# A Trainium2 kernel of attention and two mixtures of experts: routing pieces in another order, and the last slot's logits worked out from SBUF

## The chip, the cores and the metric

The kernel runs on one core of one Trainium2 chip. The metric is device time in microseconds (us). Three runs of the kernel before gave 686.45, 686.72 and 690.42 us, median 686.72. Engines: PE multiplies matrices (its weight loads, PEld, overlap), ACT, DVE and POOL do elementwise work, SP starts loads and stores. Each engine runs its instructions strictly in the order in which they are written.

## The reference

Linear attention with 128 random features, then two routed layers with one expert per token:

```
h = x @ omega.T - sum(x*x)/2          # for q and k, scaled
phi = exp(h - max(h)) / sqrt(128)
out = phi_q @ (phi_k.T @ v) / (phi_q @ sum(phi_k) + 1e-6)
# out as x [2304, 512]; then twice:
logits = x @ w_gate (+ modality_bias[modality_id] in the second)
e = argmax(logits);  gate = softmax(logits)[e]
x = gate * (relu(x @ w1[e]) @ w2[e])  # w1 [512, 1024], w2 [1024, 512], 8 experts
```

## The kernel before

Each float32 operand of a matmul is split into a hi part (a cast, on ACT, sometimes POOL) and a lo part (a subtraction, on DVE, sometimes POOL: `fp32_parts`, L40 and L41), and a product is three matmuls: hi x hi, hi x lo, lo x hi.

**Attention** runs over eight groups (a pair of batches and a pair of heads) in numbered steps. `split(gi, which, c)` (L244) makes the parts of chunk c of q or k of group gi; for group 0 the hi part is on ACT, and the lo part on DVE if the chunk is listed in FIRST, else on POOL; all later groups are on POOL. `at(step, ...)` puts a piece into a step. `st_proj` (L274) projects on PE (L283 to L285), DVE takes maxima (L287), ACT exponentials (L292: `ek` for k, `eq` for q). The pieces of MoE 1's routing run in steps of the last groups; the last batch pair's first piece is `r1_a(1)` (choice of the expert, one-hot `oh`, count `S`), after which the pools of attention are closed and those of the MoEs opened.

**Each MoE** (`moe(m)`, m = 0 and 1) sorts its tokens by expert into slots of 128 tokens: 19 slots are used in MoE 1 (18 plus the last, in `rest`), 20 in MoE 2. For a slot s of the loop PE does `layer1(s)` (24 matmuls, L819 to L821), `tx(s+1)` (transposes of the next slot's tokens into `px`, L802, whose parts are `xh`, `xl`), `layer2(s-1)` (24 matmuls, L852 to L854, with an optional piece `mid` before one of its eight steps) and `th(s)` (eight transposes of relu's result `hr` into `ht`, L835, whose parts are `hh`, `hl`). `renew` splits the next expert's weights (`w1h`, `w1l`, `w2h`, `w2l`) where a flag says that the expert changes, and loads further ones into `raw`. `gather` (L745) fetches a slot's tokens by the index `idx` on POOL's queue; a slot's result is stored by SP (MoE 1) or scattered by POOL (MoE 2).

**Routing of MoE 2** is worked out during MoE 1: `logits_v` (five experts, DVE, from PSUM, L877), `logits_g` and `logits_s` (three experts, products on POOL, L885, sums on ACT, L891); for batches of slots `r2_a` (choice), `r2_b` (ranking matmuls `pm` by `rank_mm`, L696), `r2_c` and so on. A list `todo` with `put` and `work` spreads these over the slots. `early_table` (L561) makes a short table of the first slots' tokens from `er` (the result of `early_rhs`, L529), from which the first tokens of MoE 2 are gathered. The whole table comes in pieces: `final_1` (ranks), `final_2` and `final_4` (operands `R` on DVE), `final_3` (first part of the table: indices; "payload") and `final_5` (the rest: gates and output rows).

At the end of MoE 1 a branch on `go` runs `rest`: layer 1 of MoE 2's slot 0, the last layer 2 of MoE 1 and then the logits of that slot. The next work of PE, `layer1(1, 1)`, reads parts that either side of the branch has written, so it waits until ACT and DVE have come to the end of the branch.

## Time and profile before

| what | value |
|---|---|
| median of three runs | 686.72 us |
| the profiled execution: its own time, its span | 683.77 us, 682.1 us |
| mean granted TensorE clock | 0.979 |
| PE busy | 644.0 us, 94% |
| DVE, ACT, POOL busy | 381.3, 316.0, 236.3 us |
| mean rate of the DMA engines | 107 GB/s |

In the rows further down a timeline row is: start, length, engine, line, operation, result <- operands, shape, count, and in brackets the idle time of the engine just before it with what ended it ("issue" is a wait for nothing that the profile shows, "DVEq L785" DVE's own branch). [...]

### The profile page before, as it was taken

To read this page: it belongs to the slowest core of one execution; us is meant where nothing else is said; L and a number is where in the kernel's file an instruction comes from. 1 tells how busy PE (TensorE), PEld (TensorE's weight loads), DVE (VectorE), ACT (ScalarE), POOL (GpSimd) and SP (SyncE) were. 2 spreads that over 40 slices of the span, in tenths; PEclk is the share of its full clock that TensorE was granted. 3 is DMA by queue.
4 is the path that set the end of the run, shared out by engine and by line. 5 is a ranking of instruction groups with operands and counts; after the bars stand their busy time and mean duration, and the time that the engine had idled before them with its cause. 6 is when DMAs were issued, how large, how long until landed. Compare 5 with 4: busy or idle time off the path is not lost. (4 is left out here: it accounts for less than half of the span.)

```text
span 682.1 us, 12235 instructions
## 1 busy us (share of the span) xinstructions
PE 644.0 (94%) x3764; PEld 554.9 (81%) x3764; DVE 381.3 (56%) x966; ACT 316.0 (46%) x742; POOL 236.3 (35%) x284
## 2 busy tenths in 40 slices
PE   7999999998999999999999677999999999999994
PEld 6999999886877888888888565787888888888883
DVE  3666689968587844575777468275211441564110
ACT  5666766663135734435654147212122542574231
POOL 5967665570253443523424224002121121211101
PEclk9999999998999999999999789899999999999998
DMA  6385446254165421011100801005411441550000
GB/s 201 111 268 174 140 129 217 71 181 160 39 229 193 160 85 47 32 48 47 45 27 32 297 28 36 5 32 206 152 39 42 155 157 38 170 168 19 33 17 28
DMA packets 38769, 72.64 MB, mean 107 GB/s; under 512 B 4478, under 2 KB 19966, under 8 KB 38528
## 3 DMA queue, kind: packets, MB, share of 16 engines
q1 hardware_dynamic: 33856, 57.23, 24.6%
q0 software_dynamic: 4720, 14.16, 6.3%
q8 instruction: 35, 0.57, 0.4%
q14 instruction: 78, 0.64, 0.3%
q10 hardware_dynamic: 80, 0.03, 0.0%
HBM read 55.95 MB, written 16.78 MB: 107 GB/s over the span
## 5 line engine op out<-in xcount | busy, mean ns | idle before, releaser
L819 PE MATMUL ph<-w1h,xh 128*128 128x512 f32 x312 | 127.3, 408 | 5.7 <-ACT prod L891 5.7
L852 PE MATMUL py<-w2h,hh 128*128 128x512 f32 x312 | 127.4, 408 | 0.7 <-issue 0.7
L820 PE MATMUL ph<-w1h,xl 128*128 128x512 f32 x312 | 123.6, 396 | 1.4 <-DVE xl L41 0.7
L854 PE MATMUL py<-w2l,hh 128*128 128x512 f32 x312 | 124.1, 398 | 0.0
L821 PE MATMUL ph<-w1l,xh 128*128 128x512 f32 x312 | 123.9, 397 | 0.0
L853 PE MATMUL py<-w2h,hl 128*128 128x512 f32 x312 | 123.0, 394 | 0.0
L41 DVE TENSOR_TENSOR hl<-ht,hh 128x512 fp32r<-128x512 f32 x78 | 50.3, 685 | 119.2 <-ACT hh L40 117.1
L885 POOL TENSOR_TENSOR prod<-y,wg2b 128x512 f32<-128x512 f32 x54 | 68.9, 1301 | 127.7 <-ACT prod L891 127.7
L826 ACT ACTIVATE hr<-ph 128x512 f32<-128x512 f32 x78 | 42.3, 594 | 128.2 <-PE ph L821 120.1
L860 ACT ACTIVATE y<-py,gate 128x512 f32<-128x512 f32 x36 | 24.7, 687 | 134.7 <-PE py L854 134.7
L865 POOL DMA_INDIRECT out<-y,oid x18 | 19.2, 1065 | 182.8 <-ACT y L860 178.7
L41 DVE TENSOR_TENSOR xl<-px,xh 128x512 fp32r<-128x512 f32 x40 | 27.6, 691 | 95.4 <-ACTq L785 59.5
L819 PEld LDWEIGHTS ph<-w1h,xh 128*128 128x128 f32 x312 | 59.9, 192 | 17.2 <-ACT prod L891 5.9
L877 DVE CUSTOM_DVE_ANT_0 junk<-py,wg2b,gate 128x512 f32<-128x512 f32 x95 | 71.2, 749 | 2.9 <-DVEq L785 0.2
L820 PEld LDWEIGHTS ph<-w1h,xl 128*128 128x128 f32 x312 | 60.0, 192 | 13.6 <-DVE xl L41 1.1
L821 PEld LDWEIGHTS ph<-w1l,xh 128*128 128x128 f32 x312 | 59.7, 191 | 13.3
L854 PEld LDWEIGHTS py<-w2l,hh 128*128 128x128 f32 x312 | 59.4, 190 | 13.3
L853 PEld LDWEIGHTS py<-w2h,hl 128*128 128x128 f32 x312 | 59.8, 192 | 11.9
L852 PEld LDWEIGHTS py<-w2h,hh 128*128 128x128 f32 x312 | 59.7, 191 | 11.8 <-issue 0.8
L292 ACT ACTIVATE eq<-p,mxq 128x128 f32<-128x128 f32 x144 | 41.4, 373 | 41.0 <-DVE mxq L287 41.0
L40 ACT CAST hh<-ht 128x512 fp32r<-128x512 f32 x78 | 41.8, 590 | 4.5 <-issue 4.3
L292 ACT ACTIVATE ek<-p,mxk 128x128 f32<-128x128 f32 x144 | 42.1, 392 | 3.1 <-DVE mxk L287 3.1
(227 smaller groups left out, 1127.3 us busy)
## 6 DMA issues: line engine op xcount, KB each, us to landing
raw<-w SPq DMA_DIRECT2D x56, 512.0 KB, 5.4
rawk<-kT SPq DMA_DIRECT2D x24, 192.0 KB, 3.7
rawv<-v SPq DMA_DIRECT2D x8, 576.0 KB, 5.3
rawq<-qT SPq DMA_DIRECT2D x24, 192.0 KB, 5.3
xall<-xg SPq DMA_DIRECT2D x8, 576.0 KB, 3.3
y<-y SPq DMA_DIRECT2D x18, 256.0 KB, 2.0
wg2b<-wg SPq DMA_DIRECT2D x1, 2048.0 KB, 7.0
y<-xb SPq DMA_DIRECT2D x7, 256.0 KB, 3.5
```

The lines of the kernel that those rows point to most:

```text
L40: engine_hi(hi, x)
L41: engine_lo.tensor_tensor(out=lo, in0=x, in1=hi.bitcast(F32), op=ALU.subtract)
L292: nc.scalar.activation(e[:, u], p[:, u // 2, (u % 2) * 128:(u % 2) * 128 + 128], AF.Exp, bias=mx[:, u:u + 1], scale=1.0)
L819: nc.tensor.matmul(ph[:, n], h[:, k], self.w1h[k][:, c], start=(k == 0), stop=False)
L820: nc.tensor.matmul(ph[:, n], l[:, k], self.w1h[k][:, c], start=False, stop=False)
L821: nc.tensor.matmul(ph[:, n], h[:, k], self.w1l[k][:, c], start=False, stop=(k == 3))
L826: nc.scalar.activation(r[:, n * 512:n * 512 + 512], ph[:, n], AF.Relu)
L852: nc.tensor.matmul(py, h[:, k], wh, start=(k == 0), stop=False)
L853: nc.tensor.matmul(py, l[:, k], wh, start=False, stop=False)
L854: nc.tensor.matmul(py, h[:, k], wl, start=False, stop=(k == 7))
L877: nc.vector.tensor_tensor_reduce(out=self.junk, in0=py, in1=self.wg2b[:, e], op0=ALU.mult, op1=ALU.add, scale=self.gate[0][:, s:s + 1], sc ...
L885: nc.gpsimd.tensor_tensor(out=self.prod[e - NEV], in0=y, in1=self.wg2b[:, e], op=ALU.mult)
```

## The change

At the start of attention the third split of group 0's k is written one step later, and the first split of group 1's k goes from POOL, at step 2, to ACT and DVE at step 4. The pools of attention are closed after the first part of `r1_a(1)` (it is a generator, cut by a `yield`), and the rest of it is written behind. In MoE 1 two of the four splits of w2 are written behind `th(0)`; flags and the logits of slot 0 change places, `final_2` goes to slot 1, `final_5` into the middle of a layer 2. `early_rhs` and `early_table` go some slots later, the `big` flag is loaded for fewer engines (for PE one slot later, with `go`), and `split_first` stands behind `tx(19)`. The logits of the last slot leave the branch: the new `logits_last` works out all eight on DVE from `ylast` in SBUF, behind MoE 2's `th(0)`, into `lastl`, and `r2_a(2)` adds them to the row that a one-hot `llo` picks. In MoE 2, `r2_a`, `final_1`, `final_2`, `final_3` with the gathers, and the flags each stand about one slot sooner, and `tx(4)` is at its usual place again.

The diff, cut to its core:

```diff
-        FIRST = [("k", 0), ("k", 2), ("q", 1)]
+        FIRST = [(0, "k", 0), (0, "k", 2), (0, "q", 1), (1, "k", 0)]
...
-            if gi == 0:
-
-                fp32_parts(nc, nc.scalar.copy, nc.vector if (which, c) in FIRST else nc.gpsimd, h, l, t)
+            if gi == 0 or (gi, which, c) == (1, "k", 0):
+
+                fp32_parts(nc, nc.scalar.copy, nc.vector if (gi, which, c) in FIRST else nc.gpsimd, h, l, t)
             else:
                 fp32_parts(nc, pool_copy, nc.gpsimd, h, l, t)
             parts[gi, which, c] = h, l
...
-        for c in range(3):
+        for c in range(2):
             split(0, "k", c)
...
         fill_v(0)
+        at(0, split, 0, "k", 2)
         for c in range(3):
             at(c + 1, split, 0, "q", c)
...
-                        at(s + d, split, g + 1, which, c)
+                        at(4 if (g, which, c) == (0, "k", 0) else s + d, split, g + 1, which, c)
...
+    def logits_last(self):
+
+        with self.tc.If(self.nsv > NS0):
+            for e in range(NE):
+                self.nc.vector.tensor_tensor_reduce(
+                    out=self.junk, in0=self.ylast, in1=self.wg2b[:, e], op0=ALU.mult, op1=ALU.add,
+                    scale=1.0, scalar=0.0, accum_out=self.lastl[:, e:e + 1])
+
+        if b == 2:
+
+            nl = NSLOT - NS0
+            nn = sm.tile([128, 1], F32, tag="lln", name="lln", bufs=1)
+            lo = sm.tile([128, nl], F32, tag="llo", name="llo", bufs=1)
+            lt = sm.tile([128, nl, NE], F32, tag="llt", name="llt", bufs=1)
+            nc.vector.tensor_reduce(out=nn, in_=self.kept["nb_0"], axis=AX.X, op=ALU.add)
+            nc.vector.tensor_scalar(out=lo, in0=self.i25[:, NS0:], scalar1=nn[:, 0:1], scalar2=-1.0,
+                                    op0=ALU.subtract, op1=ALU.is_equal)
+            nc.vector.tensor_tensor(
+                out=lt, in0=self.lastl.rearrange("p (o e) -> p o e", o=1).to_broadcast([128, nl, NE]),
+                in1=lo.rearrange("p (t o) -> p t o", o=1).to_broadcast([128, nl, NE]), op=ALU.mult)
+            nc.vector.tensor_tensor(out=self.lg2[:, NS0:], in0=self.lg2[:, NS0:], in1=lt, op=ALU.add)
...
-        self.all(self.r1_a(1, lgp))
+        r1 = self.r1_a(1, lgp)
+        next(r1)
         actx.close()
...
+        self.all(r1)
 
         self.moe(0)
         self.moe(1)
...
     def early_gathers(self, m):
-        self.big[m], self.bigv[m] = (self.nc.values_load(
-            self.bigi[m], engines=e, min_val=0, max_val=1, skip_runtime_bounds_check_because="a flag")
-            for e in (ALL, VEC))
+        def load(engines):
+            return self.nc.values_load(self.bigi[m], engines=engines, min_val=0, max_val=1,
+                                       skip_runtime_bounds_check_because="a flag")
+
         if m == 0:
+            self.big[m] = load(ALL)
             self.gather(m, 0, early=True)
-        else:
-            self.go = self.nc.values_load(self.goi, engines=ALL, min_val=0, max_val=1,
-                                          skip_runtime_bounds_check_because="a flag")
-        with self.tc.If(self.big[m] > 0):
+        self.bigv[m] = load(VEC)
+        with self.tc.If(self.bigv[m] > 0):
             for s in range(1 - m, NEARLY[m]):
                 self.gather(m, s, early=True)
...
             with late.Else():
-                self.layer1(m, 0, after=[lambda: split2(0, 1), lambda: self.r1_b(1), self.r1_d,
-                                         lambda: split2(2, 3)])
+                self.layer1(m, 0, after=[lambda: split2(0, 1), lambda: self.r1_b(1), self.r1_d])
                 self.tx(m, 1)
         self.th()
         if m == 0:
+            split2(2, 3)
             if_big(self.final_1, m)
+        else:
+            if_big(self.logits_last, vec=True)
         self.reload(m, 0, 1, 3)
...
-            with when(s) as there:
-                first = []
-                if (m, s) != (1, 3):
-                    first.append(lambda: self.renew(m, s + 1, 0))
-                if m == 0 and s == NS0:
-                    first.append(lambda: self.split_first(s))
-                self.layer1(m, s, after=first)
-            if m == 0 and s == NS0:
-                with there.Else():
-                    self.split_first(s)
-            if s == 4 + m:
+            with when(s):
+                self.layer1(m, s, after=[lambda: self.renew(m, s + 1, 0)])
+            if s == 5 and m == 1:
                 if_big(self.final_5, m)
-            if (m, s) == (1, 2):
-                if_big(self.final_1, m)
-            if (m, s) == (1, 3):
-                rows()
             if s > 2 * m + 1:
                 with when(s + 3):
                     self.gather(m, s + 3)
-            if (m, s) != (1, 3):
-                self.tx(m, s + 1)
-            if (m, s) == (0, 1):
+            self.tx(m, s + 1)
+            if m == 0 and s == NS0:
+                self.split_first(s)
+            if s == 1 + m:
                 if_big(self.final_2, m, vec=True)
-            if (m, s) == (1, 3):
-                flags()
-                self.renew(m, s + 1, 0)
+            if (m, s) == (1, 1):
+                if_big(self.r2_a, 2, vec=True)
+            if (m, s) == (0, 2):
+                self.logits_v(0)
             if m == 0:
                 work(s, 4.6 if 2 < s < NS0 else 0)
+                if s == NS0:
+
+                    self.big[1], self.go = (self.nc.values_load(
+                        x, engines=ALL, min_val=0, max_val=1, skip_runtime_bounds_check_because="a flag")
+                        for x in (self.bigi[1], self.goi))
 
             def renew2():
                 with when(s):
                     self.renew(m, s, 1)
 
-            self.layer2(m, s - 1, mid={(0, NS0): (4, self.tx, 1, 0), (1, 3): (6, self.tx, 1, 4)}.get((m, s)),
+            self.layer2(m, s - 1, mid={(0, NS0): (4, self.tx, 1, 0), (0, 4): (4, if_big, self.final_5, 0)}.get((m, s)),
                         after=[renew2] if s > 1 else [])
             if (m, s) == (0, 1):
                 rows()
-            if (m, s) == (1, 3):
-                self.gather(m, 6)
             with when(s):
                 self.th()
             if s == 1:
                 self.renew(m, s, 1)
             if (m, s) == (1, 1):
-                if_big(self.r2_a, 2, vec=True)
+                if_big(self.final_1, m)
             if (m, s) == (1, 2):
-                if_big(self.final_2, m, vec=True)
-            if m == 0:
+                rows()
+                self.gather(m, 6)
+            if s == 1 + m:
+                flags()
+            if m == 0 and s > 1:
                 self.logits_v(s - 1)
-            if (m, s) == (0, 1):
-                flags()
             if s in (2 + m, 3 + m):
...
                 if s == EARLY + 1:
                     put(s + 1, 2, lambda: self.all(self.first_expert(1, self.live["tot2"])))
-                    put(s + 1, 1.8, e_rhs)
-                    put(s + 1, 2.1, lambda: self.all(rhs[0]))
-                    put(s + 2, None, e_table)
+                    put(s + 3, 1.8, e_rhs)
+                    put(s + 3, 2.1, lambda: self.all(rhs[0]))
                 work(s, 0)
                 if s == NS0 - 2:
 
-                    while "er" not in self.live:
+                    while todo and todo[0][0] <= s:
                         work(s, 1e3)
                     with tc.If(self.flag(0, 5, s, [ET.SP]) < 1):
                         self.first_weights(1)
+                if s == NS0 - 1:
+                    while "er" not in self.live:
+                        work(s, 1e3)
+                    self.early_table(1, self.A2, self.live["er"], EARLY)
+                    self.early_gathers(1)
         if m == 0:
             self.logits_s(sums.pop())
             while todo:
-                work(NS0, 1e3)
-        if m == 0:
+                work(NS0 + 1, 1e3)
...
             self.layer2(m, s - 1, last=True, after=[split2] if go else [])
-            if m == 0:
-                self.logits(s - 1)
```

Three places in the order of the instructions (names as above; an `x3` is a count, an L a line, which differs by a few between the two kernels).

ACT at the start of attention, from its table load on. Before:

```order
L40 CAST hk<-rawk 128x384 x3
L292 ACTIVATE ek<-p,mxk 128x128 x6
L40 CAST hq<-rawq 128x384
L292 ACTIVATE ek<-p,mxk 128x128 x4
L40 CAST hq<-rawq 128x384
L292 ACTIVATE ek<-p,mxk 128x128 x4
L40 CAST hq<-rawq 128x384
L292 ACTIVATE ek<-p,mxk 128x128 x6
L292 ACTIVATE eq<-p,mxq 128x128 x2
```

With the change:

```order
L40 CAST hk<-rawk 128x384 x2
L294 ACTIVATE ek<-p,mxk 128x128 x2
L40 CAST hk<-rawk 128x384
L294 ACTIVATE ek<-p,mxk 128x128 x4
L40 CAST hq<-rawq 128x384
L294 ACTIVATE ek<-p,mxk 128x128 x4
L40 CAST hq<-rawq 128x384
L294 ACTIVATE ek<-p,mxk 128x128 x4
L40 CAST hq<-rawq 128x384
L294 ACTIVATE ek<-p,mxk 128x128 x4
L40 CAST hk<-rawk 128x384
L294 ACTIVATE ek<-p,mxk 128x128 x2
```

The third cast of `hk` moved behind the first exponentials, and a new cast of `hk`, that of group 1, stands behind the exponentials of step 4 and ahead of those of step 5.

PE where the ranking matmuls of MoE 2's last batch stand (`pm` from `oh` with `tri` and `ones`). Before:

```order
L819 MATMUL ph<-w1h_88,xh_68 128x512
L820 MATMUL ph<-w1h_88,xl_69 128x512
L821 MATMUL ph<-w1l_92,xh_68 128x512
L785 UNCONDITIONAL_BRANCH
L793 UNCONDITIONAL_BRANCH
L1146 COMPARE_AND_BRANCH
L703 LDWEIGHTS tri
L703 MATMUL pm<-oh_2753,tri 128x96
```

With the change:

```order
L855 MATMUL py<-w2h_2770,hh 128x512
L856 MATMUL py<-w2h_2770,hl 128x512
L857 MATMUL py<-w2l_2774,hh 128x512
L838 MATMUL ht<-ident,hr 128x128 x8
L788 UNCONDITIONAL_BRANCH
L796 UNCONDITIONAL_BRANCH
L1169 COMPARE_AND_BRANCH
L706 LDWEIGHTS tri
L706 MATMUL pm<-oh_2746,tri 128x96
L708 LDWEIGHTS ones
L708 MATMUL pm<-oh_2746,ones 128x88
```

They stood behind the layer 1 of slot 2, and now stand behind the transposes of slot 1.

DVE in slots 0 and 1 of MoE 2, from the lo part of the next tokens (`xl_69`, for slot 2) on. Before:

```order
L41 TENSOR_TENSOR xl_69<-px,xh_68 128x512
L41 TENSOR_TENSOR hl<-ht,hh 128x512 x2
L778 TENSOR_LOAD flags_132
L785 COMPARE_AND_BRANCH
L41 TENSOR_TENSOR w2l_2777<-raw_0_81,w2h_2773 128x1024
L41 TENSOR_TENSOR w2l_2778<-raw_1_82,w2h_2774 128x1024
L41 TENSOR_TENSOR w2l_2779<-raw_2_83,w2h_2775 128x1024
L41 TENSOR_TENSOR w2l_2780<-raw_3_84,w2h_2776 128x1024
L785 UNCONDITIONAL_BRANCH x2
L793 UNCONDITIONAL_BRANCH
L1146 COMPARE_AND_BRANCH
L916 TENSOR_SCALAR m_9011<-T_121 128x12
```

With the change, first behind the lo parts of slot 0, then from that `xl_69` on:

```order
L41 TENSOR_TENSOR hl<-ht,hh 128x512 x2
L1169 COMPARE_AND_BRANCH
L904 COMPARE_AND_BRANCH
L906 ISA junk,lastl<-ylast,wg2b 128x512
L906 ISA lastl 128x1
```

```order
L41 TENSOR_TENSOR xl_69<-px,xh_68 128x512
L1169 COMPARE_AND_BRANCH
L928 TENSOR_REDUCE lln<-nb_2843 128x1
L929 TENSOR_SCALAR llo<-i_99,lln 128x7
L931 TENSOR_TENSOR llt<-lastl,llo 128x56
L934 TENSOR_TENSOR lg_2758<-lg_2758,llt 128x56
L940 TENSOR_SCALAR m_8811<-T_121 128x12
L942 TENSOR_SCALAR valid_8443<-T_121 128x12
L944 TENSOR_TENSOR bi<-biasb,m_8811 128x96
```

Eight pairs of rows like the two ISA rows (the reduction and its accumulator) now stand ahead of that `xl_69`, and `r2_a`, four operations longer, ahead of the next `hl`, where it stood behind it.

## Rows read from the trace of the kernel before

**Rows 1.** The page, busy time of the engines (us, share, instructions), PE and others.

```profile
PE 644.0 (94%) x3764; PEld 554.9 (81%) x3764; DVE 381.3 (56%) x966; ACT 316.0 (46%) x742; POOL 236.3 (35%) x284
```

**Rows 2.** Busy by stretch: length, then PE, PEld, DVE, ACT, POOL; clock, DMA, GB/s.

```profile
165.70:172.30 6.60, 6.09 (x14) 4.79 (x15) 5.73 (x18) 0.35 (x2) 0.00 (x0) 0.50 0.01 2
380.70:387.30 6.60, 5.19 (x24) 4.12 (x24) 2.16 (x11) 0.00 (x0) 2.59 (x3) 0.50 1.03 357
404.60:407.60 3.00, 3.00 (x9) 2.35 (x8) 0.69 (x1) 0.22 (x1) 0.00 (x0) 0.50 0.01 3
424.95:431.60 6.65, 4.27 (x10) 3.40 (x11) 3.06 (x8) 2.52 (x6) 1.58 (x2) 0.50 0.03 10
```

**Rows 3.** Timeline of PE and ACT, start of attention.

```profile
13.75 0.39 PE L285 MATMUL p<-omh,lk 128*128 128x256 f32 x1 [0.76 <-POOL lk L41]
16.12 0.38 PE L283 MATMUL p<-omh,hk 128*128 128x256 f32 x1 [0.74 <-ACT ek L292]
...
14.89 1.69 ACT L292 ACTIVATE ek<-p,mxk 128x128 f32<-128x128 f32 x6
```

**Rows 4.** Timeline of PE, ACT and DVE, from attention to MoE 1's slot 1.

```profile
164.00 1.14 PE L835 MATMUL ht<-ident,hr 128*128 128x128 f32 x8 [2.37 <-ACT hr L826]
...
174.41 0.60 PE L802 MATMUL px<-ident,xb 128*128 128x128 f32 x4
...
159.57 3.89 ACT L40 CAST w2h<-raw 128x1024 fp32r<-128x1024 f32 x4 [6.64 <-DVE S L694]
...
157.89 0.23 DVE L461 TENSOR_TENSOR ex<-lg,mx 128x72 f32<-128x72 f32 x1
```

**Rows 5.** Timeline of PE, slots 2 to 5 of MoE 1.

```profile
195.04 0.50 PE L820 MATMUL ph<-w1h,xl 128*128 128x512 f32 x1 [0.62 <-DVEq L785]
...
213.98 0.97 PE L637 MATMUL pm<-R,A 128*128 128x100 bf16 x18 [1.14 <-DVE R L629]
```

**Rows 6.** Timeline of PE and DVE, slot 17.

```profile
381.38 0.51 PE L566 MATMUL pm<-er,A 128*128 128x28 bf16 x13 [5.45 <-DVE er L558]
...
380.97 0.36 DVE L558 TENSOR_TENSOR er<-ep,eb 128x91 bf16<-128x91 bf16 x1
382.16 0.69 DVE L41 TENSOR_TENSOR xl<-px,xh 128x512 fp32r<-128x512 f32 x1 [0.83 <-DVEq L785]
```

**Rows 7.** Timeline of PE and DVE, slot 18 to MoE 2's slot 0.

```profile
403.57 0.63 PE L802 MATMUL px<-ident,xb 128*128 128x128 f32 x4 [3.44 <-issue]
...
414.70 0.60 PE L802 MATMUL px<-ident,xb 128*128 128x128 f32 x4
...
398.24 4.63 DVE L41 TENSOR_TENSOR w1l<-raw,w1h 128x1024 fp32r<-128x1024 f32 x4 [1.30 <-ACT w1h L40]
402.78 0.68 DVE L41 TENSOR_TENSOR xl<-px,xh 128x512 fp32r<-128x512 f32 x1
```

**Rows 8.** Timeline of PE, ACT and DVE, the join behind the branch.

```profile
427.33 0.79 PE L819 MATMUL ph<-w1h,xh 128*128 128x512 f32 x1 [5.66 <-ACT prod L891]
...
429.50 1.07 ACT L40 CAST hh<-ht 128x512 fp32r<-128x512 f32 x2 [2.22 <-issue]
...
422.87 0.74 DVE L877 CUSTOM_DVE_ANT_0 junk<-py,wg2b,gate 128x512 f32<-128x512 f32 x1
...
426.71 0.08 DVE L877 DVE_READ_ACCUMULATOR2_ANT lg<- 128x1 f32 x1
```

**Rows 9.** Timeline of PE and DVE, MoE 2's slots 2 to 4.

```profile
441.69 0.47 PE L819 MATMUL ph<-w1h,xh 128*128 128x512 f32 x1
...
466.72 0.63 PE L802 MATMUL px<-ident,xb 128*128 128x128 f32 x4 [1.39 <-DMA xb<-y,idx]
...
443.81 0.17 DVE L916 TENSOR_SCALAR m<-T 128x12 f32<-128x12 f32 x1 [0.23 <-DVEq L785]
...
447.38 0.17 DVE L929 TENSOR_SCALAR valid<-valid 128x12 f32<-128x12 f32 x1
```

**Rows 10.** DMA issues of one group: tiles, queue, operation, count, median us to landing.

```profile
xb<-y,idx POOLq DMA_INDIRECT x20, 3.4
```

More of the change, by code (lines that the diff above doesn't have):

```diff
@@ L154, in consts_moe @@
         self.lg2 = c.tile([128, NSLOT, NE], F32, name="lg2")
+        self.lastl = c.tile([128, NE], F32, name="lastl")
         self.xb[1] = [c.tile([128, D], F32, name=f"xb1{i}") for i in range(4)]
@@ L163, in fill_consts_moe @@
         g.memset(self.lg2[:, NS0:], 0.0)
+        g.memset(self.lastl, 0.0)
         g.memset(self.S2[:, 0], 0.0)
@@ L1101, in start_2 @@
         with self.tc.If(self.big[1] < 1):
+            self.logits_last()
             self.r2_a(2)
@@ L1165, in moe @@
                 self.layer1(m, 0)
-                split2(0, 1, 2, 3)
+                split2(0, 1)
                 self.r1_b(1)
@@ L1244, in moe @@
                 sums.append(s - 1)
-                put(s, 0, lambda x: self.live.pop(x, None), ("y", s - 1))
+                put(s + 1, 0, lambda x: self.live.pop(x, None), ("y", s - 1))
                 b = {9: 0, EARLY + 1: 1}.get(s)
```

4 lines of the change are left out of this document (1 added, 3 removed).

## The prediction, made before the changed kernel ran

> **What bounds it.** I read the page's busy times first: the tensor engine (PE) is busy for 644 of the 682 us [rows 1], so only PE's 38 us of idle time, and PE work done at a slow clock, can be won or lost. Then the busy times by stretch, with the granted clock, around every gap of PE of over half a microsecond: four stretches run at 0.50 of full clock, 1.2 GHz in place of 2.4, each right behind a gap of 2.4 to 5.7 us [rows 2]. A matmul takes 6.09 / 14 = 0.43 us there, so 0.22 at full clock, and half of PE's busy time in such a stretch is loss: 3.0, 2.6, 1.5 and 2.1 us, 2.3 on average. Last I read the timeline around each gap for what ended it and, on the other engines, what stood ahead of that. The reader should see five places where PE waits: the start of attention [rows 3], attention to MoE 1 [rows 4], slots 2 to 5 [rows 5], the end of MoE 1 [rows 6, 7], and the join into MoE 2 with its routing [rows 8, 9]. The long stretches between are PE back to back and nothing in them changes.
>
> **Part 1, start of attention.** The ACT rows of the order show the cast of k chunk (1,k,0) behind the exponentials of step 4; before, POOL made both parts in time for PE to finish that projection at 13.75 + 0.39, after a wait of 0.76 [rows 3]. In the block of six exponentials from 14.89 the first four are step 4's (1.69 x 4/6, end near 16.0). Then cast and lo part at about 0.5 us each: 17.0, so PE ends the projection near 17.4 and reaches the next one about 18.45, where it was let in at 16.12. Part of that is slack behind the old 0.74 us wait; what is left when PE is back to back again I take as 2.2 us. PE now idles for some 4 us, and such a gap halved the clock at all four places: 2.3 more. The split of (0,k,2) one step later costs nothing: it waits for its load anyway, while the first maxima run. Sum: -4.5, bounds +1 (the cast slips in early and the waits of 0.76 and 0.74 shrink) and -6.
>
> **Part 2, into MoE 1.** ACT's four casts of w2 waited 6.64 us until 159.57 for the one-hot count of the last logits, since the attention pools closed behind the whole routing piece; the relu stood behind all four and PE's transposes waited 2.37 us for it [rows 4]. Now the pools close after the exponent's subtraction (157.89 + 0.23 = 158.1), only two casts (3.89 / 4 each) stand ahead, and they end near 160.1, before PE ends layer 1. The transposes start near 161.6 in place of 164.0, the gap is gone and with it the half clock. The lo part of x for slot 1 still stands behind two lo parts of w2 on DVE, so PE stalls there about 0.65 us and starts its second matmul near 163.3; 23 matmuls by 0.22 end at 168.3, in place of 174.41 [rows 4]. The other two casts go behind the transposes, and their lo parts end before layer 2 needs them. Gain 6.0, bounds 4 and 6.5.
>
> **Part 3, slots 2 to 5.** PE waits 0.62 us for the lo part of x behind logits and flags on DVE, and 1.14 us at the second table [rows 5]. Flags now precede the logits of slot 0, and the second table stands in the middle of a layer 2. Gain 1.7, bounds 0 and 1.8.
>
> **Part 4, end of MoE 1.** Before, the short table waited 5.45 us for its operand `er`, which DVE ended at 380.97 + 0.36 = 381.33, then layer 2 ran at half clock [rows 2, 6]. Now PE first runs that layer 2 (from 375.9, 24 x 0.22 = 5.3) and its transposes (0.8), until 382.0. `er` has the lo part of one x (0.69) and one load of a flag (0.83 idle ahead of that x before) ahead, so 382.9 [rows 6]: a wait of 0.9 stays, the table takes 0.5 [rows 6], layer 1 of slot 18 ends near 388.9. In slot 18 the splits of w1 (4.63 on DVE) stood ahead of the lo part of x, for whose bank PE's transposes of MoE 2's first tokens waited 3.44 us [rows 7]; that order is turned round. **New wait:** those tokens' gather was issued long before; now the table is copied out by DVE only behind the logits of slot 16 (the lo parts of h until an estimated 384.9, behind `er`; five reductions at (426.79 - 422.87) / 5 = 0.78 [rows 8]), so indices at 389.5, issue near 390.2, and 3.4 us to landing [rows 10]: 393.7, against 392.0 when PE is there. PE stalls 1.6 us, shorter than every gap with a half clock behind it [rows 2], so I count none. Then the lo part of x stands behind the four w1 parts, which adds 0.7. Layer 1 of MoE 2's slot 0 starts its second matmul near 398.5 and ends at 403.5; before, 414.70 [rows 7]. Gain 11.2, bounds 8 and 13.
>
> The gather moves 128 rows of 512 floats, 262 KB. [...]
>
> **Part 5, the join and MoE 2's routing.** Call Z = 427.33 - 5.66 = 421.67, when PE began to wait for the end of the branch, where ACT, DVE and POOL worked out the last slot's logits [rows 8]. Without them the branch ends with ACT's `ylast` and DVE's last lo part of w2, about Z + 1.3; 23 x 0.22 more and layer 1 of slot 1 ends at Z + 6.3; transposes of x, layer 2 (5.3) and `th` (0.8) bring PE to Z + 12.7. But the ranking matmuls stand right there now (PE rows of the order), where a layer 1 stood between, and need DVE's chain: hl of slot 0 near Z + 4.8 (ACT's 2.22 us through the branch stays [rows 8]), eight reductions from `ylast`, a flag load and lo part of x, then `r2_a`, 3.74 long from 443.81 to 447.38 + 0.17 [rows 9] and four small operations longer (about 0.95, at 0.17 to 0.26 each like its own). The reduction has no row with an operand in SBUF: bounds 0.6 (nearest DVE operation of 512 without accumulator, 0.69 [rows 7], less its read) and 0.78 [rows 8]; I take 0.78, the same instruction. So 6.2, Z + 11.4 with the branches, lo part Z + 12.8, `r2_a` Z + 17.7: a **new stall** of 5.0 us, and, as behind the old gaps [rows 2], a half clock (2.3). Before the change the next layer 1 began at 441.69, Z + 20.0 [rows 9], now at Z + 17.8 beside the ranking matmuls that both have: 2.2 won. Further on, the wait of 1.39 us for the gather at 466.72 [rows 9] becomes about 0.55, since its indices come one slot earlier and so does its use. Net 2.2 + 1.4 - 0.55 - 2.3 = +0.7, bounds -2.5 and +6 (stall and clock both absent).
>
> [...] No run here shows the reduction from SBUF.
>
> **At nothing:** the first weight reloads one slot later or earlier (their loads sit under a back-to-back PE slot of 12 us; uncovered each would cost a load's 5 us), the pool releases of y one slot later (three buffers), the smaller set of engines that load the `big` flag.
>
> **Sum.** -4.5 + 6.0 + 1.7 + 11.2 + 0.7 = 15.1 us. The profiled execution took 683.77 (span 682.1): 668.7. The median of the runs, 686.72, lies 2.95 above it, so I forecast **671.6**, from 667 to 676 if its own bounds move singly.
>
> **Rivals.** *New waits stay away.* DVE and ACT have slack that I priced as full: if the (1,k,0) cast is early enough, 4.5 come back, and if the ranking stall loses its clock fall and half its length, 4.8. For it: the old waits beside these places were under 0.8 us [rows 3]; against: both are one queue's order, and order is kept. 671.6 - 4.5 - 4.8 = 662.3; either one alone about 667. *Waits are handed on.* Each removed wait has another behind it: `er` late by 2 more, the clock falling at the gather stall too (2.3), attention at its -6, join at -2.5: 671.6 + 2 + 2.3 + 1.5 + 3.2 = 680.6, about the edge of no change. For it: four of five places get a new wait in my own account. *Slower.* The gather of MoE 2's first tokens is the one transfer newly on PE's path, issued at 390.2 while weights of the first expert may still load. PE pays 1:1 from 392.0. Landing 15 us later than reckoned, at 409, with no clock left to lose, would use up the whole gain; slower by 1% needs 22 us, at 416. Against: median 3.4 us [rows 10], and the weight loads' megabytes were issued well before.
>
> **Chances.** A measurement tells about 1% (6.9 us) from no change: faster is below 679.8, slower above 693.6. Forecast (667 to 676) 0.48; new waits away (659 to 667) 0.22; handed on (676 to 690) 0.26, of which 0.12 lies below 679.8; slower 0.04. Faster 0.48 + 0.22 + 0.12 = 0.82, same 0.14, slower 0.04. The range 661 to 682 leaves out 0.04 below and some 0.12 above (handed on beyond 682, and slower).
>
> **What would show it.** Right: PE's gaps of 2.37, 5.45, 3.44 and 5.66 us gone or under 1.7, no half clock at 165 and 381, a PE gap of 4 us near 13 with the cast of hk behind it, a gap near 5 at the ranking matmuls released by DVE's one-hot count, and the px transposes of (1,0) released by the gather. Wrong: no gap at the ranking matmuls (reductions ran early), the attention gap under 1 us, or half clock where gaps are short. A gap of over 4 us at the px transposes would mean the gather's price was missed; a clock that stays at half through attention would break the sum.

## The result, and the profile of the changed kernel

The changed kernel takes **668.27 us** (median of 4 runs, 666.96 to 670.81), the kernel before 686.59 us beside it (median of 4, 682.87 to 690.42): a ratio of 0.9737 with a 95% interval of 0.9676 to 0.9799. In a second comparison it was 667.49 us (5 runs) against 683.56 (11 runs), 0.9776 (0.9746 to 0.9806). That the kernel is faster is clear in both; whether by a full 2% is not, since the second interval reaches over 0.98. The profiled execution took 667.66 us with a span of 666.0, where that of the kernel before had 683.77 and 682.1. The time lies inside the range, 3.3 us below the forecast, and the profiled execution 1.0 below the 668.7 that the sum gave for it; the single parts are less well hit than the sum, as the following shows.

The page of the changed kernel, busy time of the engines, answers to [rows 1]:

```profile
PE 642.1 (96%) x3764; PEld 551.6 (83%) x3764; DVE 385.4 (58%) x977; ACT 314.8 (47%) x737; POOL 232.9 (35%) x280
```

PE's busy time fell by only 1.9 us, although four stretches at half clock are to be gone: something else in it became longer. The busy times by stretch (length; PE, PEld, DVE, ACT, POOL; then clock, DMA share, GB/s), behind the new gap at the start and at the places of [rows 2]:

```profile
16.40:20.00 3.60, 3.53 (x15) 3.44 (x16) 0.98 (x2) 0.64 (x3) 3.35 (x6) 0.50 0.22 56
...
165.70:172.30 6.60, 5.79 (x41) 4.34 (x40) 6.05 (x9) 5.90 (x10) 0.00 (x0) 1.00 0.77 320
382.00:389.00 7.00, 6.63 (x46) 5.46 (x44) 6.33 (x21) 3.16 (x10) 3.80 (x3) 1.00 1.04 394
404.00:408.00 4.00, 4.00 (x19) 3.22 (x18) 2.48 (x3) 3.95 (x6) 0.00 (x0) 1.00 0.04 10
424.00:431.00 7.00, 6.15 (x41) 5.13 (x41) 6.31 (x21) 0.47 (x2) 0.55 (x1) 1.00 0.10 37
```

One half clock has come, at the start; the four old ones are gone. (The rows give the clock as a share only. In the kernel before, at 0.50, ten matmuls of 512 columns start 0.426 us apart, from 167.23 to 171.49 in its PE timeline: 1.2 columns a ns, which is the prediction's 1.2 GHz as an estimate, if a column takes a cycle; its 2.4 is twice that by the share alone. At 1.00 the steady ones start 0.23 apart, 2.2 columns a ns.) PE's timeline of the changed kernel, the rows behind its gaps at the five places:

```profile
16.47 0.58 PE L285 MATMUL p<-omh,hk 128*128 128x256 f32 x1 [3.81 <-ACT hk L40]
...
167.66 1.15 PE L838 MATMUL ht<-ident,hr 128*128 128x128 f32 x8 [0.46 <-ACT hr L829]
...
382.72 0.48 PE L569 MATMUL pm<-er,A 128*128 128x28 bf16 x13 [0.37 <-DVE er L561]
...
392.88 0.63 PE L805 MATMUL px<-ident,xb 128*128 128x128 f32 x4 [0.88 <-DMA xb<-y,idx]
...
410.26 0.50 PE L822 MATMUL ph<-w1h,xh 128*128 128x512 f32 x1 [0.67 <-ACT ylast L863]
...
424.85 0.20 PE L706 MATMUL pm<-oh,tri 128*128 128x96 bf16 x1 [1.48 <-DVE oh L950]
```

The gaps of 2.37, 5.45, 3.44 and 5.66 us [rows 4, 6 to 8] have become 0.46, 0.37, 0.88 and 0.67; new are 3.81 at the start and 1.48 at the ranking matmuls. The sum of PE's gaps over 0.15 us goes from 29.0 to 15.2 us. Where PE stands at the same work in both timelines (a slot's number is that of the tokens transposed there):

| PE reaches | before | after | shift | change of it | predicted |
|---|---|---|---|---|---|
| q projection at 18.64 of before | 18.64 | 23.34 | +4.70 | +4.70 | +4.5 |
| `tx(1)`, MoE 1 | 161.00 | 166.56 | +5.56 | +0.86 | 0 |
| end of its layer 1 | 174.41 | 174.84 | +0.43 | -5.13 | -6.0 |
| slot 6's `px` | 227.09 | 225.90 | -1.19 | -1.62 | -1.7 |
| slot 18's `px` | 375.33 | 375.27 | -0.06 | +1.13 | 0 |
| `px` of MoE 2's slot 1 | 414.70 | 402.51 | -12.19 | -12.13 | -11.2 |
| `px` of its slot 5 | 474.91 | 457.42 | -17.49 | -5.30 | -0.7 |
| its last `px` | 660.77 | 644.85 | -15.92 | +1.57 | 0 |

Two rows were in no part of the sum. Between slots 6 and 18, and from slot 5 of MoE 2 on, PE waits for nothing in either kernel, yet the changed one loses 0.10 us in each slot.

### The profile page after: what moved, and what is told of

Its sections match the earlier page's. It is cut to its first block, busy times and chain, and to the rows that moved or that the text cites. A ratio compares the mean times of both kernels' runs of the same rounds, so it can differ in the third digit from the quotient of the medians.

```text
span 666.0 us, 12234 instructions
## 1 busy us (share of the span) xinstructions
PE 642.1 (96%) x3764; PEld 551.6 (83%) x3764; DVE 385.4 (58%) x977; ACT 314.8 (47%) x737; POOL 232.9 (35%) x280
## 5 line engine op out<-in xcount | busy, mean ns | idle before, releaser
L822 PE MATMUL ph<-w1h,xh 128*128 128x512 f32 x312 | 125.3, 402 | 0.7 <-ACT ylast L863 0.7
L823 PE MATMUL ph<-w1h,xl 128*128 128x512 f32 x312 | 121.8, 391 | 0.5 <-DVE xl L41 0.4
L824 PE MATMUL ph<-w1l,xh 128*128 128x512 f32 x312 | 121.9, 391 | 0.0
L824 PEld LDWEIGHTS ph<-w1l,xh 128*128 128x128 f32 x312 | 58.6, 188 | 12.7
L880 DVE CUSTOM_DVE_ANT_0 junk<-py,wg2b,gate 128x512 f32<-128x512 f32 x90 | 67.4, 749 | 2.6
```

What stands on the lines that cost most here:

```text
L822: nc.tensor.matmul(ph[:, n], h[:, k], self.w1h[k][:, c], start=(k == 0), stop=False)
L823: nc.tensor.matmul(ph[:, n], l[:, k], self.w1h[k][:, c], start=False, stop=False)
L824: nc.tensor.matmul(ph[:, n], h[:, k], self.w1l[k][:, c], start=False, stop=(k == 3))
L880: nc.vector.tensor_tensor_reduce(out=self.junk, in0=py, in1=self.wg2b[:, e], op0=ALU.mult, op1=ALU.add, scale=self.gate[0][:, s:s + 1], sc ...
```

## The experiments

Each kernel is the changed one with the edit shown, where nothing else is said. Times of one run stand beside a run of the kernel before on the same chip, or the median of its runs; what is inside a kernel is read from its own trace. Parts 3 and 4 have no run that takes them back alone: what they gave is read from the rows of the two kernels.

### The start of attention as it was (a0_start)

```diff
-        FIRST = [(0, "k", 0), (0, "k", 2), (0, "q", 1), (1, "k", 0)]
+        FIRST = [(0, "k", 0), (0, "k", 2), (0, "q", 1)]
...
-            if gi == 0 or (gi, which, c) == (1, "k", 0):
+            if gi == 0:
...
-        for c in range(2):
+        for c in range(3):
...
-        at(0, split, 0, "k", 2)
...
-                        at(4 if (g, which, c) == (0, "k", 0) else s + d, split, g + 1, which, c)
+                        at(s + d, split, g + 1, which, c)
```

> The changed kernel with the start of attention as it was before: the third split of group 0's k and the first of group 1's k at their old places and engines. Theory (the cast behind step 4's exponentials holds PE for 3.8 us, and the half clock behind it costs the rest): no PE gap over 1.5 us in the first 25 us, clock 1.00 from 16 to 22 us, everything from 24 us on some 4.7 us earlier, the span near 661.3 in place of 666.0. Rival (the delay is made up later in attention, where ACT or DVE also wait): the first transposes of MoE 1's slot 1 come less than 1.5 us earlier than 166.56 and the span is 665 or more.

Measured: 663.27 us (before 682.29), span 661.5, 4.5 less than the changed kernel. PE's timeline, and the stretch behind it:

```profile
13.96 0.38 PE L287 MATMUL p<-omh,lk 128*128 128x256 f32 x1 [0.70 <-POOL lk L41]
...
16.33 0.38 PE L285 MATMUL p<-omh,hk 128*128 128x256 f32 x1 [0.74 <-ACT ek L294]
```

```profile
16.40:20.00 3.60, 3.60 (x31) 3.60 (x32) 1.61 (x4) 2.06 (x8) 3.35 (x6) 1.00 0.02 5
```

In this run gap and half clock went with the two moved splits: the piece alone makes the kernel slower. (Of the two, the half clock did not stay away: best_a and best_b further down have this start, without the gap, and have the half clock.) `tx(1)` comes 5.06 us sooner than in the changed kernel; 0.7 of it goes again at the first gather of MoE 2, where PE now waits 1.60 us, in place of 0.88, for a transfer that does not come sooner by as much.

### What makes layer 2 slower: addresses (pad_both, pad_hh, pad_w2, before_moved)

The changed kernel has new small tiles: `lastl` (32 bytes of a partition) and `llo`, `lln`, `llt` (288 together). They shift what is placed behind them: `hh`, `hl` start at 128 in place of 352 (modulo 512 bytes), the parts of w2 at 224 in place of 416. Unused tiles shift them again:

```diff
+        self.pad1 = c.tile([128, 56], F32, name="pad1")
+        self.nc.gpsimd.memset(self.pad1, 0.0)
         self.hr = c.tile([128, FF], F32, name="hr")
...
+        self.pad2 = w2p.tile([128, 120], F32, name="pad2")
+        nc.gpsimd.memset(self.pad2, 0.0)
         self.w2h = [w2p.tile
```

This is pad_both; in pad_hh the second tile has 72 elements, so that only `hh`, `hl` are back at their old place; in pad_w2 only the second tile is there, with 48. In before_moved the kernel before gets two such tiles, of 72 and 8 elements, which put both at the places of the changed kernel.

> The changed kernel with two unused tiles, 224 bytes ahead of hr, hh and hl and 480 bytes ahead of the parts of w2, so that these operands of layer 2 lie at the same addresses modulo 512 as before the change (352 and 416, in place of 128 and 224). Nothing else differs. Theory A (layer 2 is slower by where its operands lie in SBUF): a steady layer 2 takes 5.58 to 5.60 us as before, in place of 5.69, layer 1 stays at 5.56, and the span is about 4 us shorter, near 662. Theory B (it is the order of the work beside it, or this one execution): layer 2 stays at 5.69 and the span near 666.

> As the run with two unused tiles, but only hr, hh and hl are back at their old address modulo 512 (352); w2's parts stay at 224, where the change put them. Theory A1 (the address of the stationary operand hh, hl makes layer 2 slow): a steady layer 2 takes 5.59 us. Theory A2 (that of the moving operand, w2's parts): it stays at 5.69. Theory A3 (the distance between the two): the distance modulo 64 is 0 again only if both are 32 modulo 64, which holds here, so 5.59 as well.

> The mirror of it: only w2's parts are back at their old address modulo 512 (416), while hr, hh and hl stay at 128, as the change put them. A1: layer 2 stays at 5.69 us. A2: 5.59. A3: the distance modulo 64 stays 32, so 5.69.

> The kernel before with two unused tiles (288 and 32 bytes) that put hh at 128 and w2's parts at 224 modulo 512, as in the changed kernel; the order of its instructions is untouched. Theory A (addresses): a steady layer 2 takes 5.69 us in place of 5.59, and the span is some 4 us longer than the 682.1 of before, apart from where the clock falls. Theory B (the changed order): 5.59. It also shows a second time which of the old gaps halve the clock: by the prediction's account the gaps of 2.37, 5.45, 3.44 and 5.66 us all do.

Measured, in steady slots without a gap (24 matmuls of layer 2, from the first to the transposes `ht` behind the last):

| kernel | `hh`, `hl` at | w2 at | layer 2, us | layer 1, us |
|---|---|---|---|---|
| before | 352 | 416 | 5.59 | 5.56 |
| changed | 128 | 224 | 5.69 | 5.56 |
| pad_both | 352 | 416 | 5.59 | 5.57 |
| pad_hh | 352 | 224 | 5.66 | 5.56 |
| pad_w2 | 128 | 416 | 5.68 | 5.56 |
| before_moved | 128 | 224 | 5.69 | 5.56 |
| branch_logits (below) | 352 | 448 | 5.68 | 5.58 |
| best_b (below) | 64 | 64 | 5.56 | 5.56 |

One slot in PE's timeline of the kernel before, then of before_moved, each the first matmul of a layer 2 and the transposes that follow its last:

```profile
264.37 0.48 PE L852 MATMUL py<-w2h,hh 128*128 128x512 f32 x1
...
269.96 1.03 PE L835 MATMUL ht<-ident,hr 128*128 128x128 f32 x8
```

```profile
261.52 0.48 PE L854 MATMUL py<-w2h,hh 128*128 128x512 f32 x1
...
267.21 1.03 PE L837 MATMUL ht<-ident,hr 128*128 128x128 f32 x8
```

269.96 - 264.37 = 5.59 and 267.21 - 261.52 = 5.69: the kernel before is slowed by unused bytes alone, its work in the same order. So the cause is shown in both directions, and it is worth 0.10 x 39 = 3.9 us. The untouched slots show it as well: from slot 6's `px` to slot 18's it is 148.24 us before and 148.26 in pad_both, 149.37 in the changed kernel and 149.39 in before_moved. The two places do not add up: either alone gives back 0.01 to 0.03, both together 0.10, so that none of the three theories set up for pad_hh and pad_w2 fits both. What in the addresses decides, these six placements do not tell. The whole times don't show it: pad_both had a span of 665.7 where 662 was expected, and its half clock after the start lasted until about 27 us in place of 22 (0.50 in 22 to 24 and 0.61 in 24 to 28, against 0.94 and 1.00 in the changed kernel); that is some 2.4 us of the difference, the rest is not accounted for.

### Four casts of w2 together again (cast_back)

```diff
...
-                self.layer1(m, 0, after=[lambda: split2(0, 1), lambda: self.r1_b(1), self.r1_d])
+                self.layer1(m, 0, after=[lambda: split2(0, 1), lambda: self.r1_b(1), self.r1_d,
+                                         lambda: split2(2, 3)])
...
-            split2(2, 3)
             if_big(self.final_1, m)
```

> The changed kernel with all four casts of w2 ahead of relu again, in MoE 1's slot 0; the attention pools still close early. Theory (the two casts behind the transposes are what removed the gap): the relu of slot 0 comes 1.9 us later, PE waits some 2.4 us for it and the half clock is back, so that slot 1's layer 1 ends some 5 us later than 174.84 and the span is near 671. Rival (closing the pools early did it, as the prediction had it): PE waits under 1 us more and the span is within 1.5 us of 666.

Measured: 669.54 us (before 682.29), span 667.8. PE, ACT and the stretch of cast_back, and behind them the same stretch of the kernel before, from its gap to the end of layer 1:

```profile
165.67 0.64 PE L805 MATMUL px<-ident,xb 128*128 128x128 f32 x4
...
168.66 1.15 PE L838 MATMUL ht<-ident,hr 128*128 128x128 f32 x8 [2.35 <-ACT hr L829]
...
176.20 0.60 PE L805 MATMUL px<-ident,xb 128*128 128x128 f32 x4
...
164.23 3.89 ACT L40 CAST w2h<-raw 128x1024 fp32r<-128x1024 f32 x4 [6.64 <-DVE S L697]
...
164.00:174.00 10.00, 6.90 (x46) 5.29 (x45) 8.58 (x17) 6.48 (x10) 0.00 (x0) 1.00 0.55 212
```

```profile
164.00:174.41 10.41, 9.66 (x33) 7.46 (x34) 7.43 (x20) 2.05 (x5) 0.00 (x0) 0.67 0.13 53
```

The old gap is back (2.35, before 2.37), but the half clock is not. From `tx(1)` to the end of its layer 1 it is 13.41 us before, 10.53 in cast_back, 8.28 in the changed kernel. So moving two casts is worth 10.53 - 8.28 = 2.25; the other 13.41 - 10.53 = 2.88 was the clock of that one execution. before_moved, with the old order, says the same; its PE:

```profile
160.90 0.64 PE L804 MATMUL px<-ident,xb 128*128 128x128 f32 x4
...
163.87 1.14 PE L837 MATMUL ht<-ident,hr 128*128 128x128 f32 x8 [2.34 <-ACT hr L828]
...
171.43 0.60 PE L804 MATMUL px<-ident,xb 128*128 128x128 f32 x4
```

A gap of 2.34 is there, full clock behind it (1.00 in 164 to 171), and 171.43 - 160.90 = 10.53. (Its gaps of 5.46, 3.40 and 5.67 have a slow clock behind them again: 0.50 in 381 to 384, 0.61 in 404 to 406, 0.50 in 425 to 428.) In before_moved the pools of attention close behind the whole routing piece, in cast_back ahead of `S`; the four casts stand together in both. The two times are equal, so closing the pools earlier was worth nothing.

### Does the first cast wait for the count? (late_S)

The first cast of w2 still waits 6.63 us in the changed kernel, and the row names `S`, as before, although `S` is now written behind the closing of the pools. Here two operations on an unused tile stand ahead of `S`:

```diff
+        if bp == 1:
+            d = sm.tile([128, 512], F32, tag="dmy", name="dmy", bufs=1)
+            nc.vector.memset(d, 0.0)
+            nc.vector.tensor_tensor(out=d, in0=d, in1=d, op=ALU.mult)
         self.count(oh, self.S1[:, bp], "1")
```

> The changed kernel with a fill and a product of a spare tile on DVE (about 1 us together) between the one-hot and its count S in the last routing piece, S being what the trace names as the releaser of the first cast of w2. Theory (the cast waits for the store of attention's last results to land, 3.3 us after its issue near 161.8): the cast still starts near 165.1, about 1 us ahead of S's end. Rival (the cast waits for S): it starts when S ends, near 166.1, and PE's gap at the transposes grows by about 1 us.

Measured: span 665.4 us. SP, DVE and ACT of the changed kernel, then of late_S, and last SP of the kernel before (its cast is in [rows 4], at 159.57):

```profile
155.68 6.44 SPq L392 DMA_DIRECT2D xall<-xg  x2
165.00 0.35 SPq L1047 DMA_DIRECT2D wg2b<-wg  x1
...
164.77 0.28 DVE L697 TENSOR_REDUCE S<-oh 128x8 bf16<-128x72 bf16 x1
...
165.12 2.00 ACT L40 CAST w2h<-raw 128x1024 fp32r<-128x1024 f32 x2 [6.63 <-DVE S L697]
```

```profile
154.81 6.44 SPq L392 DMA_DIRECT2D xall<-xg  x2
164.14 0.35 SPq L1051 DMA_DIRECT2D wg2b<-wg  x1
...
165.06 0.28 DVE L697 TENSOR_REDUCE S<-oh 128x8 bf16<-128x72 bf16 x1
...
164.26 1.99 ACT L40 CAST w2h<-raw 128x1024 fp32r<-128x1024 f32 x2 [6.64 <-PE ph L828]
```

```profile
150.13 6.43 SPq L390 DMA_DIRECT2D xall<-xg  x2
159.46 0.35 SPq L1022 DMA_DIRECT2D wg2b<-wg  x1
```

In late_S the cast starts at 164.26, 1.08 us before `S` ends (165.34): it does not wait for `S`. (The kernel before, where `S` ended 0.09 us ahead of the cast, was not run with a delay.) In all three kernels SP and ACT are released together (159.46 and 159.57, 165.00 and 165.12, 164.14 and 164.26), and each time the cast starts 3.0 us after the row of attention's last two stores ends (156.56, 162.12, 161.25); in cast_back (161.23 to 164.23) and a0_start (157.05 to 160.06) it is 3.0 too. A store of this group lands 3.3 us after its issue in the kernel before, 3.4 in early_gather (medians of eight in the DMA issues). So the opening of the MoEs' pools waits, by all that these rows show, for the last result of attention to be read out by its DMA. That is an inference from a constant distance; no kernel was run that changes this distance.

### The first gather of MoE 2 earlier (early_gather)

The short table is copied out ahead of the logits of slot 16, not behind them, and the gathers with it:

```diff
+            if m == 0 and s == NS0 - 1:
+                while "er" not in self.live:
+                    work(s, 1e3)
+                self.early_table(1, self.A2, self.live["er"], EARLY)
+                self.early_gathers(1)
             if m == 0 and s > 1:
                 self.logits_v(s - 1)
...
-                if s == NS0 - 1:
-                    while "er" not in self.live:
-                        work(s, 1e3)
-                    self.early_table(1, self.A2, self.live["er"], EARLY)
-                    self.early_gathers(1)
```

> The changed kernel with the short table, its copy on DVE and the gathers of MoE 2's first tokens written ahead of the logits of slot 16, which the prediction had named as what makes the gather late. Theory (DVE's five reductions, 3.9 us, stand ahead of the indices): the first gather is issued about 4 us earlier than 389.42, PE's wait of 0.88 us at the px transposes vanishes, and the logits of slot 16 end 1 us later with nobody waiting: MoE 2 starts some 0.9 us earlier. Rival (the gather is late for another reason, the transfer shares the DMA engines with the weights of the first expert): the wait stays over 0.5 us though the issue is earlier.

Measured: 669.41 us (before 687.55), span 667.6. POOL, PE and DVE of early_gather, then the same work of the changed kernel:

```profile
385.01 1.04 POOL L753 DMA_INDIRECT xb<-y,idx  x1 [10.28 <-DMA raw<-w]
389.98 3.79 POOL L888 TENSOR_TENSOR prod<-y,wg2b 128x512 f32<-128x512 f32 x3
...
391.91 0.63 PE L805 MATMUL px<-ident,xb 128*128 128x128 f32 x4 [0.47 <-DMA xb<-y,idx]
398.92 0.50 PE L823 MATMUL ph<-w1h,xl 128*128 128x512 f32 x1 [2.47 <-DVEq L788]
...
390.91 7.35 DVE L41 TENSOR_TENSOR w1l<-raw,w1h 128x1024 fp32r<-128x1024 f32 x4 [0.23 <-ACT w1h L40]
```

```profile
389.42 1.04 POOL L753 DMA_INDIRECT xb<-y,idx  x1 [1.75 <-issue]
...
391.80 4.63 DVE L41 TENSOR_TENSOR w1l<-raw,w1h 128x1024 fp32r<-128x1024 f32 x4 [0.23 <-DMA raw<-w]
```

Issued 4.4 us earlier, the gather spares PE only 0.4 us of its wait: it takes until about 391.9, 6.9 us from its issue, while weights fill the DMA engines (share 1.03, 391 GB/s in 384 to 388). And PE gets a new wait of 2.47 us for `xl`, since DVE's four lo parts of w1 take 7.35 us in place of 4.63: POOL's products (389.98 to 393.77, of them 2.86 us behind the start of the lo parts), which the gathers have pushed back, run beside them. Both read two operands from SBUF. The 2.72 us added are close to the 2.86 us of the overlap. In best_b (below), where the products stand well ahead of the same four lo parts (379.79 to 383.60, the lo parts from 389.80), these take 4.63 again. That the products are the cause is read from these rows; no kernel was run that moves them alone.

### The last slot's logits in the branch again (branch_logits)

```diff
-        if b == 2:
-            nl = NSLOT - NS0
...
-            if_big(self.logits_last, vec=True)
...
             self.layer2(m, s - 1, last=True, after=[split2] if go else [])
+            if m == 0:
+                self.logits(s - 1)
```

> The changed kernel with the last slot's logits back in the branch at the end of MoE 1, by DVE, POOL and ACT as before, and without the four operations that add them in. Theory (taking them out is what the join won, and the stall at the ranking matmuls is its price): PE waits some 5.6 us for the end of the branch in place of 0.67, mostly with a half clock behind it, the 1.48 us at the ranking matmuls are gone, and from the end of MoE 1 to MoE 2's third transposes (402.51 to 457.42 in the changed kernel, 54.9 us) it takes 58 to 61. Rival (the old wait was hidden in what follows): 56 or less. The removed tile also moves hh to 352 and w2's parts to 448 modulo 512, so a layer 2 may take 5.59 to 5.69.

Measured: 672.45 us (before 683.56), span 670.7, 4.7 more than the changed kernel. PE at the join of branch_logits:

```profile
415.11 0.80 PE L822 MATMUL ph<-w1h,xh 128*128 128x512 f32 x1 [5.67 <-ACT prod L894]
```

The old gap stands there to 0.01 us, and the clock falls (0.69 in 409 to 420). From the `px` of slot 1 to that of slot 2 it is 20.08 us against 13.78; of these 6.3 the slots behind it, without a wait at the ranking matmuls, give 1.9 back, so that 4.4 stay at the `px` of slot 5. Its layer 2 goes at 5.68, so the addresses have no part in this.

### Three runs more (best_a, best_b, changed_again)

best_a joins what the runs had shown: the start of attention as before, `hh` and w2 at 352 and 416 by unused tiles, and the copy of the short table, without the gathers, ahead of the logits of slot 16. best_b differs from it in the tiles alone, of 112 and 104 elements. The piece of the table in both, then the difference of the two:

```diff
+            if m == 0 and s == NS0 - 1:
+                while "er" not in self.live:
+                    work(s, 1e3)
+                self.early_table(1, self.A2, self.live["er"], EARLY)
             if m == 0 and s > 1:
                 self.logits_v(s - 1)
...
                 if s == NS0 - 1:
-                    while "er" not in self.live:
-                        work(s, 1e3)
-                    self.early_table(1, self.A2, self.live["er"], EARLY)
                     self.early_gathers(1)
```

```diff
-        self.pad1 = c.tile([128, 56], F32, name="pad1")
+        self.pad1 = c.tile([128, 112], F32, name="pad1")
...
-        self.pad2 = w2p.tile([128, 120], F32, name="pad2")
+        self.pad2 = w2p.tile([128, 104], F32, name="pad2")
```

> The changed kernel with three things put together: the start of attention as before, hh and w2's parts at their old addresses modulo 512 (352 and 416), and the short table with its copy on DVE ahead of the logits of slot 16, while POOL's products keep their place ahead of the gathers. From the single runs: 4.5 + 39 x 0.10 + up to 0.9 us: the span near 657 in place of 666.0, the ratio to the kernel before 0.96. If the gains overlap (a gather met earlier waits longer, as where the start alone was put back) 658 to 659.5.

> The same as best_a, but hh and w2's parts both at 64 modulo 512, which is where layer 1's operands lie in every kernel here, whose 24 matmuls and steps take 5.56. Theory (a layer goes at the speed of its operands' addresses): layer 2 takes 5.56 to 5.59, the span up to 1.2 us under best_a. Rival (it hangs on something else, such as what DVE and ACT read and write beside it): 5.65 or more.

> The changed kernel itself once more, beside the two above: its ratio to the kernel before, 0.974 at first, within 0.968 to 0.980; layer 2 at 5.69 us again, and 3.8 us of waiting at the start of attention. The length of the half clock behind that wait may differ (6.7 us at first).

Measured against 683.56 us before: best_a 664.22 (6 runs), ratio 0.9710 (0.9675 to 0.9745); best_b **662.59** (5 runs), 0.9696 (0.9664 to 0.9728); the changed kernel again 667.49, 0.9776 (0.9746 to 0.9806). best_b beats both kernels; against best_a its lead is not clear, as the intervals overlap. Its layer 2 at 5.56 us came as expected, but best_a's span of 662.2 missed the expected 657 to 659.5. Two of the pieces gave less than they should. The clock (0.50 in 18 to 22) fell at the start in both, behind gaps of 1.10, 0.75 and 0.73 us (best_b), though in the kernel before (1.44, 0.76 and 0.74) and in a0_start (1.24, 0.70 and 0.74) the gaps at these places had full clock behind them (1.00 in 16 to 22). And the early table cost time here; PE and DVE of best_b:

```profile
389.67 0.63 PE L806 MATMUL px<-ident,xb 128*128 128x128 f32 x4 [1.69 <-DVE xl L41]
395.08 0.50 PE L824 MATMUL ph<-w1h,xl 128*128 128x512 f32 x1 [0.93 <-DVEq L789]
...
381.15 1.22 DVE L594 TENSOR_TENSOR idx<-ti,T 128x4 int32<-128x4 f32 x1
```

That `idx` takes 0.16 us in the changed kernel; here POOL's products (379.79 to 383.60) run beside it. The two waits are 2.62 us where the changed kernel has 0.88. That the table is the reason is read from these rows; a best_b without this piece was not run.

## Why the prediction was right or wrong

**Part 1, start of attention: right** (+4.70 for +4.5). ACT in the changed kernel:

```profile
14.85 1.17 ACT L294 ACTIVATE ek<-p,mxk 128x128 f32<-128x128 f32 x4
15.86 0.56 ACT L40 CAST hk<-rawk 128x384 fp32r<-128x384 f32 x1
```

The cast starts at 15.86 behind the four exponentials, where 16.0 was reckoned, and the half clock came; a0_start takes both away. Between there and `tx(1)` another 0.86 is lost, not foreseen: 0.57 of it is a wait for MoE 1's first gather at 148.30, which a0_start and the kernel before don't have.

**Part 2, into MoE 1: right in direction, wrong in mechanism** (5.13 for 6.0). The failed step is "now the pools close after the exponent's subtraction": it rests on the releaser that [rows 4] name, `S`. In the changed kernel late_S shows that the cast does not wait for `S`, though the row still names it; the casts waited as long as ever, and cutting `r1_a` in two gave nothing (10.53 us in cast_back as in before_moved). The second half of the step was right: with two casts ahead of it the relu comes sooner, PE waits 0.46 us in place of 2.37, and 2.25 us are won. The rest is the half clock, which the sum took as sure behind such a gap, and which two kernels with the same gap did not have.

**Part 3, slots 2 to 5: right.** Both waits, 0.62 and 1.14 us, are gone: 1.62 us, and nearly 2.0 with the slower layer 2 taken out (four slots by 0.10), against 1.7 and a bound of 1.8; the 0.3 beyond the two waits are not accounted for.

**Part 4, end of MoE 1: right, a little low** (12.13 for 11.2, inside 8 to 13). Both waits that were named are there with the releasers named, at 0.37 for 0.9 (`er`, at 382.67 for 382.9) and 0.88 for 1.6 (the gather; indices at 388.65 for 389.5). The stall for the lo part of x of 0.7 is not to be found. The account closes: between the `px` of slot 18 and that of MoE 2's slot 1 PE's waits fell from 9.62 us (5.45, 0.73, 3.44) to 1.24, and the half clocks, 2.6 and 1.5 by the prediction's own reckoning, are gone. That is 12.5, from which the slower layer 2 takes some 0.3. early_gather shows that the order chosen is not improved by this earlier gather.

**Part 5, the join: the term that was mis-sized** (5.30 for 0.7, inside its own -2.5 to +6). The new wait is at the ranking matmuls, as said, but 1.48 us long, not 5.0, and no half clock stands behind it. DVE in the changed kernel, where PE's wait behind the branch began at 409.59, which is the prediction's Z here:

```profile
412.71 1.29 DVE L41 TENSOR_TENSOR hl<-ht,hh 128x512 fp32r<-128x512 f32 x2 [1.83 <-ACTq L788]
413.92 0.68 DVE L906 CUSTOM_DVE_ANT_0 junk<-ylast,wg2b 128x512 f32<-128x512 f32 x1
...
419.67 0.08 DVE L906 DVE_READ_ACCUMULATOR2_ANT lastl<- 128x1 f32 x1
...
424.54 0.26 DVE L950 TENSOR_TENSOR oh<-oh,valid 128x96 bf16<-128x96 bf16 x1
```

PE needs `oh`, whose end at 424.80 is Z + 15.2, and not the end of `r2_a`, for which the chain was carried to Z + 17.7. Of these 2.5 us, 0.4 are an earlier `hl`, 0.4 the reductions ((419.75 - 413.92) / 8 = 0.73 each, where 0.78 was taken; the upper of its two bounds), 0.8 the load of the flag and the branches, and 0.9 lie in `r2_a`, two of whose operations stand behind `oh`. PE for its part came 1.1 later (Z + 13.8 for Z + 12.7), mostly since a matmul was reckoned at 0.22 where the steady rows give 0.23 to 0.24. 5.0 - 2.5 - 1.1 = 1.4. The 2.3 for the clock hung on the same length, and behind 1.48 us the clock stayed at 1.00. With both put right the prediction's own sum is 2.2 + 2.5 + 1.4 - 0.55 = 5.55, against 5.30. branch_logits gives the worth of the piece as 4.4 us. On the reduction from SBUF: measured are 0.73 us against 0.785 from PSUM, from one to the next, so about 0.055 less each. The rows from PSUM also take `gate`, and no run separates the two.

**The term that was not there.** "The long stretches between are PE back to back and nothing in them changes" was wrong: 39 layer 2's by 0.10, 3.9 us, for tiles that no one counts as work. It hides the better outcome of part 5 almost wholly: by the table parts 1 to 5 and the 0.86 behind part 1 give -18.6 and the two drifts +2.7, together -15.9, against 16.1 in the spans; the other 1.2 of the 3.9 lie inside the parts. That the sum of 15.1 came so close is luck in part: part 5 and part 4 came 4.6 and 0.9 better than forecast, part 1 with what follows it, part 2 and the drifts 1.1, 0.9 and 2.7 worse.

**Rivals.** Of "New waits stay away" the half about the ranking stall came true, the half about the cast did not. "Waits are handed on" did not come: each wait that was removed has another behind it, but a small one. The gather of "Slower" landed within 0.9 us of PE's need; early_gather shows its price in a busy stretch, 6.9 us for a median of 3.4, so that rival had 3.5 us less distance than it seemed, out of the 15 that it needed. Of the signs named for "right" the gap near 5 at the ranking matmuls is the only one that did not come at its size.

## What to carry to other kernels

Trace a wait to the instruction that the reader needs, not to the end of the piece that holds it, and test a named releaser by delaying it before building on it. Price a fall of the clock as a chance, from the gaps at which it came and those at which it did not. When a change adds even a few bytes of on-chip tiles, compare the steady pace of the untouched loops, and try a few placements of their operands.

## What the runs showed of the hardware that was not expected

- The same 24 matmuls with 128x512 operands take 5.56 (best_b), 5.59 (before, pad_both), 5.66 (pad_hh), 5.68 (pad_w2, branch_logits) or 5.69 us (changed, before_moved), according to the placement of `hh`, `hl` and the parts of w2 in SBUF, at full clock and without a gap. Why is open.
- Equal gaps of PE need not give equal clocks, and a half clock came without a long gap too. Behind 2.37 us at 164 it was 0.67 on average in the kernel before, behind 2.34 and 2.35 at the same place 1.00 in two others (before_moved, cast_back); behind 1.10, 0.75 and 0.73 us at the start 0.50 in best_b, 1.00 behind 1.24, 0.70 and 0.74 in a0_start. In early_gather the matmuls of 256 columns slow down at 11.5 us (0.12 us apart before, 0.21 behind it; 0.50 in 12 to 16), behind a wait of 1.45, and the long wait at the start, 14.0 to 16.71, began only after that. One kernel differs from run to run as well: best_a took 666.57 us at a mean clock of 0.986, 660.94 and 661.32 at 0.997.
- Four subtractions on DVE took 7.35 us in early_gather in place of 4.63 (changed, best_b), and an operation on 128x4 numbers 1.22 in best_b in place of 0.16 (changed), while POOL multiplied operands from SBUF. That POOL is the cause is not shown by a run of its own.
